# Moving the four copies of kept scores within the even steps of a fused top-k attention and MLP kernel

## The chip, the cores and the metric

The kernel runs on one core of one Trainium2 chip (trn2). The metric is the device time of one execution in microseconds (us). The engines are called PE (TensorE, matrix products), DVE (VectorE), ACT (ScalarE), POOL (GpSimd) and SP (SyncE, which issues most DMAs here). PEld is PE's loading of weights. Each engine works through its own queue in order; semaphores hold an instruction until what it needs is there.

## The reference

Two blocks follow one another: attention in which each query keeps its 32 best keys, and a two-layer MLP.

```python
# q, k, v: (8, 8, 576, 64)
scores = scale * np.matmul(q, k.transpose(0, 1, 3, 2))
kth = np.partition(scores, -top_k, axis=-1)[..., -top_k:-top_k + 1]   # top_k = 32
scores = np.where(scores >= kth, scores, -1000000000.0)
scores = scores - np.max(scores, axis=-1, keepdims=True)
attn = np.exp(scores)
attn = attn / (np.sum(attn, axis=-1, keepdims=True) + 1e-09)
attn_out = np.matmul(attn, v)
# x: the heads side by side, (4608, 512)
h = x @ w_in                    # (512, 2048)
out = np.maximum(0.01 * h, h) @ w_out   # (2048, 512)
```

## The kernel before

**Units and steps.** A unit is 128 query rows for two heads (one pair), or 64 rows of two pairs where the 576 queries leave a rest. It has 2 x 576 scores in each of 128 partitions. There are 144 units, one to a step. The first four steps stand beside the loading of weights; from step 4 on, `even(s)` and `odd(s + 1)` alternate, and everything an engine does in them is issued in the order in which these two functions name it. Nothing is reordered by a planner; only the amount of MLP work in a slot (`mlp_steps(budget)`) is shared out by a cost count.

**The life of a unit.** In a step, `cur` is the unit of this step, `old` that of the step before, `older` the one before that.
- PE computes the scores of two units at a time at the end of an even step (`scores`, L237) into three PSUM tiles: two of name `wide` (352 keys of each unit) and one of name `narrow` (224 keys of both). ACT moves them to `s_sb` in the odd step (`keep_scores_of`, L246, four copies).
- DVE runs `top_k(cur)`: two elementwise operations (L310), then four rounds of MAX8 (L316) and MATCH_REPLACE8 (L321). They give the 32nd largest score of a row.
- One step later come `limits` (L331 on ACT, L332 and L333 on POOL) and `mask` (L337, ACT), then `exponents` (L340, ACT), which also sum, and `sums` (L345, `ze`). DVE takes the reciprocal `rz` (`reciprocals`, L349). ACT multiplies by it (`normalize`, L352).
- In an even step the unit before last (`older`) is normalized after the masks of `old`, and `old` itself later in the same step, after the exponentials.
- POOL takes the 32-bit weights apart into 16-bit halves (`split`, L361); SP writes the halves to DRAM (L362, twice) and reads them back transposed as `wT` (`transpose`, L366, a DMA that waits for both L362 to have landed).
- PE multiplies `wT` with the values (`values`, L405) into a spare part of a `wide` tile; ACT puts the result into `x` (L428). `x` feeds the MLP, whose pieces on PE are L445, L462, L544, L558 and L636, and whose results leave PSUM by ACT's L440, L464, L532 and L566, called by `catch_up` where the MLP's work is cut.

**Kept scores.** In the odd steps 5 to 15, `score_early` lets PE compute scores of units that come much later, from keys and queries loaded into `raw` tiles (`load_early`, L271, L276). They use the same three PSUM tiles. In the following even step, four copies on ACT (L285) bring them to SBUF and four DMAs on SP (L286) to DRAM; `fetch_scores` (L301) brings them back much later. Two functions matter here:

```python
281    def store_scores(count):
282        for _ in range(min(count, len(to_store))):
283            u, k0, k1, ps = to_store.pop(0)
284            one = raws.tile([P, 2, WIDE], F32, name="top", bufs=2)[:, :, 0:k1 - k0]
285            nc.scalar.copy(one, ps)
286            nc.sync.dma_start(kept_of[u].rearrange("p (i n) -> p i n", i=2)[:, :, k0:k1], one)
...
216    def tiles_for_scores(us):
218        narrow = ps_sc.tile([P, 2, 512], F32, name="narrow")
221            wide = ps_sc.tile([P, 2, 512], F32, name="wide", bufs=2)
```

The four copies of a step are, in order, `wide`, `narrow`, `narrow`, `wide`; here they are called copies 1 to 4. `top` has two buffers, so copy 3 uses the buffer of copy 1 and copy 4 that of copy 2. `scores(new, ...)` at the end of the same even step writes the PSUM tiles that the copies read: its order is first `wide` tile, `narrow` (16 matmuls), second `wide` tile.

In `even`, before: `store_scores(2)` stands at line 801, after the masks, and again at line 816, after `sums(old)`. The units with kept scores are those of steps 6, 8, 10, 12, 14 and 16 as far as copying goes; in the other even steps both calls find nothing to store.

Of the kernel before, what the change touches and what calls it, by code (L numbers as in the profile page):

```python
# [20 lines left out]
def kernel(  # L21
# [160 lines left out]
    def load_waiting():  # L182
        if waiting_v or waiting:
            nc.sync.dma_start(*(waiting_v or waiting).pop(0))
# [31 lines left out]
    def tiles_for_scores(us):  # L216

        narrow = ps_sc.tile([P, 2, 512], F32, name="narrow")
        ps, spare = {}, []
        for k, u in enumerate(us):  # L220
            wide = ps_sc.tile([P, 2, 512], F32, name="wide", bufs=2)
            ps[u] = ((wide[:, :, 0:WIDE], 0, WIDE),
                     (narrow[:, :, k * NARROW:(k + 1) * NARROW], WIDE, S))
            spare.append(wide[:, :, WIDE:WIDE + P])
        return ps, spare
# [55 lines left out]
    def store_scores(count):  # L281
        for _ in range(min(count, len(to_store))):
            u, k0, k1, ps = to_store.pop(0)
            one = raws.tile([P, 2, WIDE], F32, name="top", bufs=2)[:, :, 0:k1 - k0]
            nc.scalar.copy(one, ps)  # L285
            nc.sync.dma_start(kept_of[u].rearrange("p (i n) -> p i n", i=2)[:, :, k0:k1], one)  # L286
# [11 lines left out]
    def fetch_scores(u):  # L298
        u.both = work.tile([P, 2, S], F32, name="s_sb", bufs=5)
        u.s = [u.both[:, i, :] for i in range(2)]  # L300
        nc.sync.dma_start(u.both.rearrange("p i n -> p (i n)"), kept_of[u])  # L301

    def top_k(u):

        u.tops = small.tile([P, 2, ROUNDS, 8], F32, name="tops")
        pairs = work.tile([P, 2, 2, HS], F32, name="pairs", bufs=1)
        for n, op in enumerate((ALU.max, ALU.min)):
            nc.vector.tensor_tensor(pairs[:, :, n, :], u.both[:, :, 0:HS], u.both[:, :, HS:S], op)  # L310
        yield
        for r in range(ROUNDS):
            rest = [pairs[:, i, 0, :] if r < ROUNDS // 2 else
                    pairs[:, i, :, :].rearrange("p n h -> p (n h)") for i in range(2)]
            for i in range(2):
                nc.vector.max(out=u.tops[:, i, r, :], in_=rest[i])  # L316
            if r == ROUNDS - 2:
                yield
            if r + 1 < ROUNDS:
                for i in range(2):  # L320
                    nc.vector.match_replace(out=rest[i], in_to_replace=u.tops[:, i, r, :],  # L321
                                            in_values=rest[i], imm_value=LOWEST)
            yield

    def limits(u):

        largest, least_kept = u.tops[:, :, 0, 0], u.tops[:, :, ROUNDS - 1, 7]
        u.nleast = small.tile([P, 2], F32, name="nleast")
        u.nbias = small.tile([P, 2], F32, name="nbias")
        u.z = small.tile([P, 2], F32, name="z")  # L330
        nc.scalar.activation(u.nleast, least_kept, AF.Copy, bias=0.0, scale=-1.0)  # L331
        nc.gpsimd.tensor_tensor(u.nbias, least_kept, largest, ALU.subtract)  # L332
        nc.gpsimd.tensor_scalar(u.nbias, u.nbias, SCALE, None, ALU.mult)  # L333

    def mask(u, i):

        nc.scalar.activation(u.s[i], u.s[i], AF.Prelu, bias=u.nleast[:, i:i + 1], scale=1.0, alpha=BELOW)  # L337

    def exponents(u, i):
        nc.scalar.activation(u.s[i], u.s[i], AF.Exp, bias=u.nbias[:, i:i + 1], scale=SCALE,  # L340
                             accum_out=u.z[:, i:i + 1])
# [5 lines left out]
    def reciprocals(u):  # L347
        u.rz = small.tile([P, 2], F32, name="rz")
        nc.vector.reciprocal(u.rz, u.ze)  # L349

    def normalize(u, i):
        nc.scalar.activation(u.s[i], u.s[i], AF.Copy, bias=0.0, scale=u.rz[:, i:i + 1])  # L352

    def split(u):


        pairs = u.both.rearrange("p i n -> p (i n)").bitcast(U16).rearrange("p (n h) -> p n h", h=2)
        u.apart = halves.tile([P, 2, 2 * S], U16, name="apart")
        for h in range(2):
            split = work.tile([P, 2 * S], U16, name="split", bufs=2)  # L360
            nc.gpsimd.tensor_copy(split, pairs[:, :, h])  # L361
            nc.sync.dma_start(u.apart[:, h, :], split)  # L362

    def transpose(u):
        u.wT = work.tile([P, 2 * NKC - 1, P], F32, name="wT", bufs=3)
        nc.sync.dma_start_transpose(out=u.wT.bitcast(U16), in_=u.apart.rearrange("p h n -> (p h) n"))  # L366

    def transpose_in_haste(u):

        both = u.both.rearrange("p i n -> p (i n)")  # L370
        u.parts_T = []
        for c0, c1 in ((0, 8), (8, 2 * NKC - 1)):
            pt = ps_sc.tile([P, 2, 512], F32, name="wide", bufs=2)
            pt = pt.rearrange("p h (c n) -> p (h c) n", n=P)
            for c in range(c0, c1):
                nc.tensor.transpose(pt[:, c - c0, :], both[:, c * P:(c + 1) * P], ident)
            u.parts_T.append((c0, c1, pt))
# [113 lines left out]
    def send_now():  # L491
        while to_send:
            nc.sync.dma_start(*to_send.pop(0))
# [18 lines left out]
    def catch_up():  # L512
        while due:
            due.pop(0)()
# [143 lines left out]
    def mlp_steps(budget):  # L658
        owed[0] += budget
        while owed[0] > 0:  # L660
            if running[0] is None:
                if not ready:
                    owed[0] = 0.0
                    return
                running[0] = mlp(ready.pop(0))
            cost = next(running[0], None)
            if cost is None:
                running[0] = None
            else:
                owed[0] -= cost  # L670
                backlog[0] -= cost
# [12 lines left out]
    def unit(n):  # L684
        return steps[n] if FIRST <= n < len(steps) else None
# [15 lines left out]
    def slot_budget(s):  # L701

        after = [at for at, _ in ready_at if at > s]
        if len(after) >= len(CHUNKS) - EARLY:
            return EARLY_SHARE * (0.6 if s - 2 in HASTY else 1.0)
        until = after[0] if after else s + 1
        group = [GROUP * (at % 2 == 0 and at < len(steps)) for at in range(s, until)]
        return max((backlog[0] + sum(group)) / len(group) - group[0], 0.0) / SLOTS
# [5 lines left out]
    with tc.manual_schedule():  # L714
# [67 lines left out]
        def even(s):  # L782
            cur, old, older = unit(s), unit(s - 1), unit(s - 2)
            in_haste = s - 2 in HASTY
            new = [u for u in steps[s + 2:s + 4] if u]
            if new and new[0] in early_units:
                new = []
            picks = top_k(cur) if cur else iter(())
            budget = slot_budget(s)
            next(picks, None)  # L790
            if older:
                reciprocals(older)
            for _ in range(4):
                next(picks, None)
            load_waiting()
            send_now()
            if old:
                limits(old)
                mask(old, 0)
                mask(old, 1)  # L800
            store_scores(2)
            catch_up()
            if older:
                normalize(older, 0)
                normalize(older, 1)
                if not in_haste:
                    split(older)
                    transpose(older)
                else:
                    transpose_in_haste(older)  # L810
            mlp_steps(budget)
            if old:
                exponents(old, 0)
                exponents(old, 1)
                sums(old)
            store_scores(2)
            if older and in_haste:
                keep_transposed(older)
            if old:
                reciprocals(old)  # L820
            for _ in picks:
                pass
            for _ in range(4):
                mlp_steps(budget)
            if old:
                normalize(old, 0)
                normalize(old, 1)
            sum_now(2)
            mlp_steps(budget)
            mlp_steps(budget)  # L830
            if unit(s + 3) in early_units:
                fetch_scores(unit(s + 3))
            ps, spare = tiles_for_scores(new) if new else (None, [])
            weighed = values(s, spare)
            if new:
                scores(new, ps)
            load_more(s)
            return new, ps, weighed
# [221 lines left out]
```

## Time and profile before

| | us |
|---|---|
| median of 3 runs | 1443.55 (1441.15 to 1444.76) |
| profiled execution | 1442.51 |
| its span | 1440.7 |
| mean granted PE clock | 0.981 |

| L285 and L286, the copies of kept scores and their DMAs | |
|---|---|
| L285 copies | 12 `wide` of 0.75, 12 `narrow` of 0.53, from 125.8 to 225.6 us |
| L286 DMAs | 24, from 126.5 to 231.3 us, 2.8 us from issue to landing in the median (2.5 to 3.7) |

How to read the profile's lines: a timeline line gives the start in us from the span's start, the duration, the engine, the line of the kernel, the operation, what is written <- what is read, and the count; in brackets the idle time of the engine just before, and what ended it. SPq is SP's queue issuing a DMA. A line of the waits names engine, tile and line that waited, what released it, the total in us, the times, and the longest. A busy share is a mean over stages with different limits; a wait's price is read in its own stage.

### The profile page before, as it was taken

To read this page: it belongs to the slowest core of one execution; us is meant where nothing else is said; L and a number is where in the kernel's file an instruction comes from. 1 tells how busy PE (TensorE), PEld (TensorE's weight loads), DVE (VectorE), ACT (ScalarE), POOL (GpSimd) and SP (SyncE) were. 2 spreads that over 40 slices of the span, in tenths; PEclk is the share of its full clock that TensorE was granted. 3 is DMA by queue.
4 is the path that set the end of the run, shared out by engine and by line. 5 is a ranking of instruction groups with operands and counts; after the bars stand their busy time and mean duration, and the time that the engine had idled before them with its cause. 6 is when DMAs were issued, how large, how long until landed. Compare 5 with 4: busy or idle time off the path is not lost.

```text
span 1440.7 us, 27849 instructions
## 1 busy us (share of the span) xinstructions
PE 1350.1 (94%) x9794; PEld 1031.2 (72%) x9794; DVE 1321.4 (92%) x3412; ACT 1025.3 (71%) x2144; POOL 714.3 (50%) x796
## 2 busy tenths in 40 slices
PE   5679799969999999999999999999999999999998
PEld 2234454438778888878788888878778888888887
DVE  7989998999999999999999999999999999999700
ACT  6877877767677777767777777767677777777621
POOL 2332335435646464655555555555655555555512
PEclk9899899989999999999999999999999999999999
DMA  7683766665767656675676567766765565555400
GB/s 301 229 269 114 221 181 191 180 182 132 190 182 170 159 141 188 184 199 128 197 196 179 142 146 182 201 178 151 201 176 165 149 159 143 167 141 139 127 12 15
DMA packets 410239, 241.64 MB, mean 168 GB/s; under 512 B 340080, under 2 KB 356977, under 8 KB 408177
## 3 DMA queue, kind: packets, MB, share of 16 engines
q1 hardware_dynamic: 408944, 238.80, 60.5%
q8 instruction: 77, 1.26, 0.4%
q10 hardware_dynamic: 1152, 1.05, 0.2%
q14 instruction: 66, 0.53, 0.1%
HBM read 55.77 MB, written 100.27 MB: 108 GB/s over the span
## 4 chain that ended last, share of the span: by engine, by line
DVE 67%; PE 19%; issue 6%; ACT 4%; DMA 2%; POOL 1%; DVEq 0%; SPq 0%; POOLq 0%
DVE tops L316 32%; DVE pairs L321 25%; DVE pairs L310 7%; PE ph L544 5%; PE pz L558 4%; PE ph L445 3%; PE wide L405 2%; PE pz L636 1%; PE wide L237 1%; DVE rz L349 1%; ACT s_sb L340 1%; ACT s_sb L352 1%; DMA apart<-split 1%; PE narrow L237 1%; DMA wT<-apart 1%
## 5 line engine op out<-in xcount | busy, mean ns | idle before, releaser
L316 DVE MAX8 tops<-pairs 128x8 f32<-128x288 f32 (+1 forms) x1152 | 636.6, 593 | 0.3 <-DVE rz L349 0.3
L544 PE MATMUL ph<-x,w_in 128*128 128x256 f32 x2048 | 458.5, 383 | 7.8 <-ACT gT L532 6.9
L321 DVE MATCH_REPLACE8 pairs<-tops,pairs 128x288 f32<-128x288 f32 (+1 forms) x864 | 460.9, 539 | 0.0
L544 PEld LDWEIGHTS ph<-x,w_in 128*128 128x128 f32 x2048 | 384.8, 190 | 86.5 <-issue 16.3
L361 POOL COPY split<-s_sb 128x1152 uint16<-128x1152 uint16 x284 | 317.5, 1147 | 206.1 <-ACT s_sb L352 206.1
L352 ACT ACTIVATE s_sb<-s_sb,rz 128x576 f32<-128x576 f32 x288 | 207.0, 767 | 140.7 <-DVE rz L349 139.9
L332 POOL TENSOR_TENSOR nbias<-tops 128x2 f32<-128x2 f32 x144 | 73.8, 513 | 385.2 <-DVE tops L316 381.6
L558 PE MATMUL pz<-w_out,gT 128*128 128x256 f32 x1024 | 226.8, 379 | 0.8 <-POOL gT L483 0.8
L310 DVE TENSOR_TENSOR pairs<-s_sb 128x576 f32<-128x576 f32 x288 | 214.4, 784 | 12.4 <-ACT s_sb L261 2.0
L340 ACT ACTIVATE s_sb<-s_sb,nbias 128x576 f32<-128x576 f32 x288 | 223.6, 784 | 0.0
L558 PEld LDWEIGHTS pz<-w_out,gT 128*128 128x128 f32 x1024 | 194.2, 190 | 28.4 <-POOL gT L483 2.0
L337 ACT ACTIVATE s_sb<-s_sb,nleast 128x576 f32<-128x576 f32 x288 | 207.6, 768 | 4.7
L405 PE MATMUL wide<-wT,vt 128*64 128x128 f32 (+1 forms) x2560 | 157.0, 284 | 24.9 <-DMA wT<-apart 22.2
L405 PEld LDWEIGHTS wide<-wT,vt 128*64 128x64 f32 (+1 forms) x2560 | 128.5, 138 | 62.9 <-issue 39.0
L558 PE MATMUL pz<-raw,top 128*128 128x256 f32 x512 | 116.6, 383 | 3.5 <-ACT o_sb L566 3.5
L558 PEld LDWEIGHTS pz<-raw,top 128*128 128x128 f32 x512 | 95.4, 190 | 24.9 <-issue 4.7
L237 PE MATMUL wide<-kt,qt 64*64 64x352 f32 x1040 | 101.6, 461 | 0.0
L246 ACT COPY s_sb<-wide 128x704 f32<-128x704 f32 x130 | 99.1, 762 | 3.2 <-PE wide L237 3.2
L532 ACT ACTIVATE gT<-ph 128x512 f32<-128x512 f32 x128 | 75.4, 589 | 32.8 <-PE ph L544 32.8
L333 POOL TENSOR_SCALAR nbias<-nbias 128x2 f32<-128x2 f32 x144 | 84.4, 586 | 12.6
L331 ACT ACTIVATE nleast<-tops 128x2 f32<-128x2 f32 x144 | 28.6, 199 | 86.8 <-DVE tops L316 85.9
L566 ACT COPY o_sb<-pz 128x256 f32<-128x256 f32 x112 | 41.9, 374 | 67.3 <-PE pz L558 67.2
(76 smaller groups left out, 1257.3 us busy)
## 6 DMA issues: line engine op xcount, KB each, us to landing
apart<-split SPq DMA_DIRECT2D x284, 288.0 KB, 2.2
raw<-in_weights_dram SPq DMA_DIRECT2D x15, 1024.0 KB, 6.2
vt<-in_vk_dram SPq DMA_DIRECT2D x32, 320.0 KB, 3.7
qt<-in_qT_dram SPq DMA_DIRECT2D x32, 288.0 KB, 3.5
kt<-in_kT_dram SPq DMA_DIRECT2D x32, 288.0 KB, 4.0
out_dram<-o_sb SPq DMA_DIRECT2D x64, 128.0 KB, 2.4
s_sb<-kept SPq DMA_DIRECT2D x12, 576.0 KB, 4.3
kept<-top SPq DMA_DIRECT2D x12, 352.0 KB, 2.9
```

Of the source, the lines that this page charges most:

```text
L237: nc.tensor.matmul(to[r0:r0 + LEFT, i, :], qt[d, q0 - left:q0 - left + LEFT], kt[d, k0:k1], start=True, stop=True)
L246: nc.scalar.copy(u.both[:, :, k0:k1], to)
L310: nc.vector.tensor_tensor(pairs[:, :, n, :], u.both[:, :, 0:HS], u.both[:, :, HS:S], op)
L316: nc.vector.max(out=u.tops[:, i, r, :], in_=rest[i])
L321: nc.vector.match_replace(out=rest[i], in_to_replace=u.tops[:, i, r, :], in_values=rest[i], imm_value=LOWEST)
L337: nc.scalar.activation(u.s[i], u.s[i], AF.Prelu, bias=u.nleast[:, i:i + 1], scale=1.0, alpha=BELOW)
L340: nc.scalar.activation(u.s[i], u.s[i], AF.Exp, bias=u.nbias[:, i:i + 1], scale=SCALE, accum_out=u.z[:, i:i + 1])
L352: nc.scalar.activation(u.s[i], u.s[i], AF.Copy, bias=0.0, scale=u.rz[:, i:i + 1])
L361: nc.gpsimd.tensor_copy(split, pairs[:, :, h])
L405: nc.tensor.matmul(po[n * D:(n + 1) * D, side, 0:P], v_of[u.pairs[0]][k, at, side, :], u.wT[k, at + side * NKC if at + 1 < NKC else at, :] ...
L544: nc.tensor.matmul(ph[:, i, 0:n], w_in[c][:, f * P:(f + 1) * P], x[:, c, 0:n], start=(c == 0), stop=(c == HP - 1),)
L558: nc.tensor.matmul(to, g[:, f, :], w(f), start=(first and f == 0), stop=(f == HALF - 1), skip_group_check=not first)
```

## The change

Two calls of `store_scores(2)` remain, in other places. The one behind the masks is taken out. The one behind `sums(old)` stays, and now carries copies 1 and 2. A new one stands at the end of the even step, after `normalize(old)`, the last MLP slots and `fetch_scores`, ahead of `tiles_for_scores(new)`, and carries copies 3 and 4. Copies, sizes, buffers and tiles are as before.

```diff
@@ -798,7 +798,6 @@
                 limits(old)
                 mask(old, 0)
                 mask(old, 1)
-            store_scores(2)
             catch_up()
             if older:
                 normalize(older, 0)
@@ -830,6 +829,7 @@
             mlp_steps(budget)
             if unit(s + 3) in early_units:
                 fetch_scores(unit(s + 3))
+            store_scores(2)
             ps, spare = tiles_for_scores(new) if new else (None, [])
             weighed = values(s, spare)
             if new:
```

In the changed program's order of instructions, PE, DVE and POOL have the same sequence as before. On ACT the L285 move as said. On SP the four L286 of a step stand together, behind the two L362 and the L366 of the even step; before, two stood ahead of these and two behind.

## Prediction

> **What bounds the kernel now.** I read the page first: engine totals, then the chain of work that ended last, then the list of who waited for whom on VectorE (DVE), then the timeline of the stretch that the change touches.
>
> ```profile
> PE 1350.1 (94%) x9794; PEld 1031.2 (72%) x9794; DVE 1321.4 (92%) x3412; ACT 1025.3 (71%) x2144; POOL 714.3 (50%) x796
> ...
> DVE 67%; PE 19%; issue 6%; ACT 4%; DMA 2%; POOL 1%; DVEq 0%; SPq 0%; POOLq 0%
> ```
>
> ```profile
> DVE rz L349 <- ACT ze L345: 21.2, 11, 8.0
> ```
>
> Two thirds of the chain is DVE's top-k. From about 300 us the chain is an unbroken run of L316/L321 pairs (one step each 8.8 us) until DVE has no more work, then TensorE (PE) drains to the end at 1440.7. In 300 to 320 us PE itself idles for the transposed weights, so PE follows DVE there: a delay of DVE ahead of 300 us moves everything behind it. What DVE waits for is almost only `rz`, the reciprocal, on ScalarE's (ACT) `ze`. The copies of kept scores (L285) run only in the even steps 6, 8, 10, 12, 14 and 16, between 125 and 232 us. Step 6, in the timeline:
>
> ```profile
> 125.75 0.75 ACT L285 COPY top<-wide 128x704 f32<-128x704 f32 x1 [2.52 <-PE wide L237]
> ...
> 128.93 2.23 POOL L361 COPY split<-s_sb 128x1152 uint16<-128x1152 uint16 x2 [6.51 <-ACT s_sb L352]
> ...
> 130.10 1.44 SPq L362 DMA_DIRECT2D apart<-split  x2
> ...
> 130.52 0.52 ACT L285 COPY top<-narrow 128x448 f32<-128x448 f32 x1
> 130.64 0.17 DVE L349 RECIPROCAL rz<-ze 128x2 f32<-128x2 f32 x1 [1.65 <-ACT ze L345]
> ...
> 133.43 2.60 SPq L366 DMA_TRANSPOSE wT<-apart  x1
> ...
> 136.12 1.20 SPq L286 DMA_DIRECT2D kept<-top  x2
> ```
>
> See two things. First, copy 1 stands ahead of the exponentials and waits 2.52 for PE; DVE then waits 1.65 for `ze`. Second, SP's queue is in order: copies 3 and 4 ended at 131.6, but their stores (L286) were issued at 136.12, when the transpose (L366) ahead of them, itself waiting for the split to land, had gone. In step 8 even the first stores stood behind a transpose:
>
> ```profile
> 143.21 2.58 SPq L366 DMA_TRANSPOSE wT<-apart  x1
> ...
> 145.84 1.24 SPq L286 DMA_DIRECT2D kept<-top  x2
> ...
> 148.85 0.53 ACT L285 COPY top<-narrow 128x448 f32<-128x448 f32 x1 [1.04 <-DMA kept<-top]
> ```
>
> Copy 3 writes the buffer of copy 1 (`top` has two), and started 3.0 us after copy 1's store was issued: ACT waited for a DMA.
>
> **What the change removes.** No instruction is added or dropped; PE, DVE and POOL keep their order, ACT and SP change theirs. Copies 1 and 2 leave the place ahead of `ze`. DVE's mid-step waits for `ze` in the six steps are 1.65, 0, 0, 0.30, 1.35 and 3.15: 6.45 us at most to be won. In step 6: the matmuls for L440 end at 124.93, so L440 and the two L352 (0.49 + 1.44) end at 126.9 instead of 128.9, `ze` at 128.6, and DVE, free at 128.99, waits for nothing. What is late next is below.
>
> **What it moves onto the path.** On SP the order becomes L362 x2, L366, then all four L286. So every first store now stands behind a transpose, as in step 8. Call N the end of the older unit's two normalizations (L352) in an even step. From N to the L286 behind that transpose the six steps of before took 7.25, 7.45, 7.18, 6.97, 7.17 and 7.12 us: 7.2. The landing of such a store is 2.5 to 3.7, and 3.0 and 2.8 where a first store stood behind a transpose: 2.9, and 0.1 for the start. Copy 3 thus starts at N + 10.2, though ACT is there at about N + 5 (exponentials and `ze` 1.75, copies 1.3, L352 1.45). Copies 3 and 4 take 0.53 + 0.75: over at N + 11.5.
>
> Queued behind copy 3 on ACT: the odd step's `nleast` and masks (1.65 by 133.38 to 134.98), L428 and the four L246, the exponentials, `ze`. On PE: scores(new) needs the `narrow` bank (copy 3) and the second `wide` bank (copy 4); PE came to it at 132.94 in step 6 and now waits until about 137.6. Its 16 + 8 matmuls end by N + 12.5, before ACT reads them, so PE is not the longer arm. DVE waits for that `ze` at the next even step's `rz`. From the first of L428/L246 to the end of `ze` the odd steps took 4.48, 4.27, 4.42, 4.78, 4.28, 4.77; in the fourth and sixth an L440 of 0.5 stands ahead. So `rz` follows at N + 17.5 to 18.5. Then ACT needs `nleast`, masks and L352 (3.1) to the next N; two L440 add 1.1 from step 10 to 12, the sends at L628 and an L440 add 2.05 from 14 to 16. From N to N: 20.7, 20.5, 21.8, 21.5, 22.6, against 17.65 that DVE's two steps take. ACT and SP now set the pace, and DVE idles 3 to 5 us in each double step.
>
> **The sum.** N in step 6 is 126.9; adding up, step 16 has 234.0, and `rz` at the start of step 18 comes at 234.0 + 18.5 = 252.5. Before:
>
> ```profile
> 240.08 0.17 DVE L349 RECIPROCAL rz<-ze 128x2 f32<-128x2 f32 x1 [0.59 <-ACT ze L345]
> ```
>
> That is +12.4 us; the waits of before in this stretch are replaced by the longer loop, so the gain is already in it. From step 18 there are no copies, and PE, ACT and DVE are late by 12.0 to 12.6 alike, so later waits stay. Profiled execution: 1442.5 + 12.4 = 1454.9 (span 1440.7 and 1.8 around it). It lies 1.0 under the median of the runs, 1443.55, which gives 1455.9. I say **1455.5**.
>
> **Unknown sizes.** How copy 3 waits is not in this order in the trace. If no wait came, all six waits would be won: -6.45. With the fastest rows (6.97 and 2.5) a step is 0.6 shorter: +8.8; with the slowest (7.45 and 3.7) 1.05 longer: +18.7. I take the middle because the 7.2 repeats within 0.3. Later, DVE's waits of 1.85 and 0.50 at 287 and 299 us could be won if PE comes there relatively earlier: -2.4. The DVE adds at 248 us, stretched to 4.77 for two beside a POOL addition (1.43 elsewhere), could meet POOL otherwise: 3.3 either way. The other reordered pieces (gT copies, L440, loads at the end of the step) cost nothing: ACT idles 5 us ahead of copy 3, and loads are due steps later; without that cover each costs its 0.5.
>
> **Clock.** PE will idle about 4 us per even step. In this trace an idle of 3.75 us at 152 to 156 was followed by half clock:
>
> ```profile
> 148.00:150.00 2.00, 2.00 (x34) 1.00 1.02 373
> ...
> 156.00:158.00 2.00, 1.99 (x19) 0.50 1.06 399
> ...
> 164.00:166.00 2.00, 2.00 (x22) 0.50 0.65 240
> ```
>
> (Columns: window, busy PE, granted clock, DMA share, GB/s.) The 38 matmuls of L405 took 4.31 instead of 2.34. Scores at half speed end 1.5 us later, still hidden: ACT reads `narrow` at N + 13.9. From scores(new) of step 10 to those of step 12 PE has 19.7 us of work in 21.8, so there a slow clock shows: 0 to 4 us in all. I keep 0 for the forecast and 4 for the range. The Trainium skill, "TensorE: Matmul & The Clock Gate", Part 1, says that the clock halves after an idle window of about 3.4 us whose grid runs freely, so that a gap of 4 us may or may not meet one; as an estimate by that page, one window per gap would be 1.7 us of PE time each, 10 in all, mostly inside PE's slack. The trace's 156 us case agrees with a halving; no row shows how often it will happen.
>
> A rule speaks for the change: the skill's "Trainium Kernel Development and Optimization", Best Practices, wants double buffering to overlap DMA with compute, and `top` is double-buffered. By that rule alone the stores would be hidden and the sum would be -6.45; the 1.04 at 148.85 shows two buffers not to be enough when the store's issue is held up.
>
> **Rivals.** (1) *Faster*: copy 3 does not wait. The mechanism is the earlier `ze`: DVE wins 1.65, 0.30, 1.35 and 3.15, and the end comes at 1436 to 1437. It decides if the first stores land before N + 5; for it speaks that in steps 12 to 16 of before no store was behind a transpose, against it the order of SP's queue in the changed program. Chance 0.06. (2) *Absorbed*: the wait exists but ACT's idle time, 29% of the span, swallows most. For 0 to +6 copy 3 would have to start 1.1 to 2.1 us earlier than N + 10.2 (12.4 over six steps is 2.1 each), or part is won back at 248 to 300 us: 1443 to 1449. Chance 0.12, of which 0.05 within 0.3%. (3) *Worse*: PE at half clock reaches scores(new) after ACT. If each stall brings three slow windows, as at 156 to 171 (10.2 us slow, 5.1 lost), it passes PE's slack by 5 at step 12 and 1 or so elsewhere: +8 on top, 1463 to 1466. Chance 0.12. (4) Forecast, +6 to +20: 0.70.
>
> **How the numbers follow.** The range 1448.5 to 1463 is the forecast with the bounds (+8.8 - 2.4, and +18.7, and 1.0 between profile and median), and leaves out about 0.2. Some 0.3% (4.3 us) is what a measurement here can tell from no change: faster 0.06, same 0.05, slower 0.89.
>
> **What would show it.** ACT's L285 waiting for "DMA kept<-top" six times, about 5 us each, where before has one of 1.04. PE waiting for L285 at `narrow` L237, about 4 us, six times. DVE's wait for `ze` gone in mid-step and 3 to 5 us at each even step's first `rz`, the total at 30 to 36 instead of 21.2; step 18's `rz` near 252.5. After 300 us, the same pattern shifted. I am wrong if L285 shows no DMA wait, if L286 is issued ahead of L366, or if the shift at 300 us is not that at the end.

## The result, and the profile after

The changed kernel takes 1458.71 us in the median of 5 runs (1457.56 to 1460.76), before 1443.55 (1441.15 to 1444.76): ratio 1.0109, 95% interval 1.0094 to 1.0124. The profiled execution took 1458.71 with a span of 1456.9, so 16.2 more than the 1440.7 of before. The forecast was 1455.5, range 1448.5 to 1463.

The page of the changed kernel, engine totals and chain by engine:

```profile
PE 1354.6 (93%) x9794; PEld 1032.2 (71%) x9794; DVE 1320.1 (91%) x3412; ACT 1025.2 (70%) x2144; POOL 711.0 (49%) x796
...
DVE 65%; PE 16%; issue 6%; ACT 6%; DMA 4%; POOL 2%; SPq 1%; ACTq 0%; DVEq 0%; POOLq 0%
```

DVE and ACT do no more work than before (1321.4 and 1025.3 there). PE's 4.5 us more for the same 9794 matmuls are slower matmuls: the mean granted clock of this execution is 0.978 instead of 0.981. What is new is in the chain: ACT 6% instead of 4, DMA 4% instead of 2, and SP's queue with 1%. Who waited for whom (total, times, longest):

```profile
DVE rz L349 <- ACT ze L345: 29.4, 14, 8.0
...
ACT top L285 <- DMA kept<-top: 28.7, 8, 5.5
...
PE narrow L237 <- ACT top L285: 12.6, 4, 4.4
PE wide L405 <- ACT top L285: 5.3, 1, 5.3
...
DVE pairs L310 <- ACT s_sb L246: 12.0, 7, 2.9
```

The copies wait 28.7 us for DMAs, where before has 1.0 in all. DVE's waits for ACT (L349 and L310 together) are 41.4 instead of 22.4. Step 6 in the timeline of the changed kernel:

```profile
125.38 1.43 ACT L352 ACTIVATE s_sb<-s_sb,rz 128x576 f32<-128x576 f32 x2
...
128.60 0.17 DVE L349 RECIPROCAL rz<-ze 128x2 f32<-128x2 f32 x1 [0.32 <-ACT ze L345]
...
129.10 0.54 ACT L285 COPY top<-narrow 128x448 f32<-128x448 f32 x1
...
131.40 2.51 SPq L366 DMA_TRANSPOSE wT<-apart  x1
...
134.00 1.26 SPq L286 DMA_DIRECT2D kept<-top  x2
...
136.97 0.53 ACT L285 COPY top<-narrow 128x448 f32<-128x448 f32 x1 [5.51 <-DMA kept<-top]
137.56 1.56 PE L237 MATMUL narrow<-kt,qt 64*64 64x224 f32 x16 [4.12 <-ACT top L285]
...
140.99 1.43 DVE L310 TENSOR_TENSOR pairs<-s_sb 128x576 f32<-128x576 f32 x2 [2.19 <-ACT s_sb L246]
...
144.79 0.17 DVE L349 RECIPROCAL rz<-ze 128x2 f32<-128x2 f32 x1 [2.38 <-ACT ze L345]
```

Read it downwards. The first line ends at N, 126.81 here. The wait of 1.65 in mid-step shrank to 0.32: that is the gain. Then the two stores leave SP at 134.00, right behind the transpose, though their copies had ended at 129.6; copy 3 starts when the first has landed, 5.5 us after ACT was ready; PE and DVE wait in turn. The end of the same story, the first `rz` of step 18:

```profile
255.01 0.17 DVE L349 RECIPROCAL rz<-ze 128x2 f32<-128x2 f32 x1 [1.89 <-ACT ze L345]
```

The stretch can be measured by itself: from the first `rz` of step 6 (122.93 before, 122.21 after) to that of step 18 it takes 117.15 us before and 132.80 after, +15.65. That leaves 0.6, as a balance, for the whole rest of the span. Since this start scatters from 121.8 to 125.3 in the profiles, with the loading of weights ahead of it, the stretch is what the runs below are compared by, called S. S is read in one execution of each kernel, and PE's clock enters it too, as is seen at e10.

### The profile page after: what moved, and what is told of

It reads as the page before. It is cut to its first block, busy times and chain, and to the rows that moved or that the text cites. A ratio compares the mean times of both kernels' runs of the same rounds, so it can differ in the third digit from the quotient of the medians.

```text
span 1456.9 us, 27857 instructions
## 1 busy us (share of the span) xinstructions
PE 1354.6 (93%) x9794; PEld 1032.2 (71%) x9794; DVE 1320.1 (91%) x3412; ACT 1025.2 (70%) x2144; POOL 711.0 (49%) x796
## 4 chain that ended last, share of the span: by engine, by line
DVE 65%; PE 16%; issue 6%; ACT 6%; DMA 4%; POOL 2%; SPq 1%; ACTq 0%; DVEq 0%; POOLq 0%
DVE tops L316 31%; DVE pairs L321 24%; DVE pairs L310 7%; PE ph L544 4%; PE pz L558 4%; PE ph L445 2%; PE wide L405 2%; PE pz L636 1%; DMA apart<-split 1%; DMA raw<-in_weights_dram 1%; DMA kept<-top 1%; ACT s_sb L340 1%; PE wide L237 1%; POOL split L361 1%; ACT s_sb L246 1%
## 5 line engine op out<-in xcount | busy, mean ns | idle before, releaser
L310 DVE TENSOR_TENSOR pairs<-s_sb 128x576 f32<-128x576 f32 x288 | 212.9, 779 | 23.2 <-ACT s_sb L246 12.0
L405 PE MATMUL wide<-wT,vt 128*64 128x128 f32 (+1 forms) x2560 | 156.8, 284 | 27.1 <-DMA wT<-apart 20.7
L405 PEld LDWEIGHTS wide<-wT,vt 128*64 128x64 f32 (+1 forms) x2560 | 128.6, 138 | 64.6 <-issue 39.7
L246 ACT COPY s_sb<-wide 128x704 f32<-128x704 f32 x130 | 99.2, 763 | 1.8 <-PE wide L237 1.8
L331 ACT ACTIVATE nleast<-tops 128x2 f32<-128x2 f32 x144 | 28.7, 199 | 81.9 <-DVE tops L316 80.9
```

Source lines behind the costliest of these rows:

```text
L246: nc.scalar.copy(u.both[:, :, k0:k1], to)
L405: nc.tensor.matmul(po[n * D:(n + 1) * D, side, 0:P], v_of[u.pairs[0]][k, at, side, :], u.wT[k, at + side * NKC if at + 1 < NKC else at, :] ...
```

## The experiments

The theory: copy 3 waits for its buffer, that is for the store of copy 1, and this store stands on SP's in-order queue behind the transpose. Rival 1: the late place of copies 3 and 4 hurts by itself (PSUM is free later, the odd step starts later on ACT). Rival 2: copies 1 and 2 behind `ze` hold the `wide` bank, and so the weighted values and PE's clock. Each ratio is to runs of the kernel before on the same chip.

**Four places instead of two, no order changed (e1_own_buffers).** Copies 2 and 3 share one buffer, copy 4 goes to columns of `gT` that are idle until 358 us.

```diff
-            one = raws.tile([P, 2, WIDE], F32, name="top", bufs=2)[:, :, 0:k1 - k0]
+            n = stored[0] % 4
+            stored[0] += 1
+            keep = kept_of[u].rearrange("p (i n) -> p i n", i=2)[:, :, k0:k1]
+            if n == 3:
+                one = gT[:, 0:8, P:P + WIDE // 4].rearrange("p (i a) n -> p i a n", i=2)
+                ps = ps.rearrange("p i (a n) -> p i a n", a=4)
+                keep = keep.rearrange("p i (a n) -> p i a n", a=4)
+            elif n == 0:
+                one = raws.tile([P, 2, WIDE], F32, name="top", bufs=2)
+            else:
+                if n == 1:
+                    two[0] = raws.tile([P, 2, 2, NARROW], F32, name="top", bufs=2)
+                one = two[0][:, n - 1]
             nc.scalar.copy(one, ps)
-            nc.sync.dma_start(kept_of[u].rearrange("p (i n) -> p i n", i=2)[:, :, k0:k1], one)
+            nc.sync.dma_start(keep, one)
```

> The changed kernel, with four places for the four copies of an even step: copy 1 in one top buffer, copies 2 and 3 in the two halves of the other, copy 4 in columns of gT that nothing uses before 358 us. Orders on all queues stay those of the changed kernel. Theory (copy 3 waits for the store of copy 1, which stands on SP behind the transpose): the 28.7 us that ACT waits at the copies for DMA go to about 0, copy 3 starts at N + 5 instead of N + 10.2 (N: end of the older unit's normalization), the first rz of step 18 comes 12 to 16 us earlier than 255.0, and the time is 1437 to 1444. Rival 1 (the place at the end of the even step is what hurts: PSUM is free later and the odd step's ACT work starts later, whatever the DMA does): 1450 to 1459. Rival 2 (copies 1 and 2 behind ze hold the wide bank, and with it the weighted values and TensorE's clock): still above 1452.

Measured: 1441.70, ratio 0.9976 (0.9964 to 0.9988); S 117.41. Copy 3 in step 6, with N at 128.74 (`kernel.py` is 13 lines longer here, so L285 is L298):

```profile
133.27 0.54 ACT L298 COPY top<-narrow 128x448 f32<-128x448 f32 x1
```

It starts at N + 4.5, with no idle time ahead of it. No copy waits for a DMA any more, and that alone takes the whole loss away, with every queue in the order of the changed kernel. Rival 1 falls: copies 3 and 4 stand as late as before the edit. Rival 2 has something left, one wait of 6.5 us of PE for copy 1 at L405, but it does not make the kernel slower than before.

**The transpose behind the first stores (e8_transpose_behind).** SP's queue alone changes.

```diff
                     split(older)
-                    transpose(older)
...
             store_scores(2)
+            if older and not in_haste:
+                transpose(older)
             if older and in_haste:
```

> The changed kernel with one thing moved on SP's queue alone: the even step's transpose is issued behind the stores of copies 1 and 2 instead of ahead of them. ACT, PE, DVE and POOL keep the changed kernel's order. Theory: the first store is issued at about N + 3 and lands by N + 6, so copy 3 waits about 1 us instead of 5; the transpose itself, which waits for the split to land at N + 4.5, is not late; the time is 1438 to 1446. Rival 1 and rival 2: no instruction of ACT has moved, so 1452 to 1459.

Measured: 1438.73, ratio 0.9964 (0.9952 to 0.9976); S 114.22. Its timeline in step 6, and its waits:

```profile
134.06 1.27 SPq L286 DMA_DIRECT2D kept<-top  x2
...
135.92 2.67 SPq L366 DMA_TRANSPOSE wT<-apart  x1
...
136.90 0.53 ACT L285 COPY top<-narrow 128x448 f32<-128x448 f32 x1 [0.94 <-DMA kept<-top]
```

```profile
ACT top L285 <- DMA kept<-top: 4.5, 6, 1.2
```

The stores now leave ahead of the transpose. N is 131.3 here, so the transpose starts at N + 4.6, as early as in before, and copy 3 starts at N + 5.6 instead of N + 10.2. The wait of 28.7 has become 4.5. Buffers, copies and ACT's order are those of the changed kernel: SP's order is the cause. And this version is faster than the kernel before.

**One half of the change alone (e2_second_move): copies 1 and 2 behind the masks, 3 and 4 at the end of the step.**

```diff
                 mask(old, 1)
+            store_scores(2)
             catch_up()
...
                 sums(old)
-            store_scores(2)
```

(against the changed kernel)

> One half of the change alone: copies 1 and 2 stay behind the masks, copies 3 and 4 go to the end of the even step. The first stores then stand on SP ahead of the split and the transpose of the older unit. Theory: copy 3 finds its buffer free but for step 8, where an earlier transpose stands ahead; VectorE's mid-step waits of before (1.65, 0.30, 1.35, 3.15) stay; 1441 to 1447. Rival 1 (the late place hurts by itself): 1450 or more. Rival 2 (the first pair's move hurts): as before, 1443 plus or minus 2, so it is not told from the theory here.

Measured: 1442.58, ratio 0.9995 (0.9985 to 1.0004); S 118.91. No copy waits for a DMA, since the first stores now stand ahead of the split. DVE's mid-step waits stay, 3.40, 0, 0, 2.18, 1.34 and 3.14; the first is 1.8 longer than in before, behind half clock (0.50 from 106 to 108 us) that before did not have there; the fourth is 1.9 longer, and why was not looked for. The second move alone neither wins nor loses.

**The other half alone (e3_first_move): all four copies behind `ze`.**

```diff
                 sums(old)
-            store_scores(2)
+            store_scores(4)
...
-            store_scores(2)
             ps, spare = tiles_for_scores(new) if new else (None, [])
```

(against the changed kernel)

> The other half alone: copies 1 and 2 go behind ze as in the changed kernel, and copies 3 and 4 stay where they were before, right behind ze. Theory: copy 3 again waits for a store that stands behind the transpose, until N + 10.2, and now the normalization of the old unit (1.45) stands behind it on ACT as well, so the loop gets some 1.5 us longer in each of six steps: 1462 to 1470. Rival 1 (the end of the step is what hurts): not slower than before by more than 2, 1440 to 1446. Rival 2: 1452 to 1459, as the changed kernel.

Measured: 1484.03, ratio 1.0278 (1.0262 to 1.0294); S 157.72. Much slower, and 14 to 22 more than the theory had said. The timeline in step 12 tells why:

```profile
207.86 0.53 ACT L285 COPY top<-narrow 128x448 f32<-128x448 f32 x1 [6.56 <-DMA kept<-top]
...
209.13 0.60 ACT L440 ACTIVATE scale<-ph 128x512 f32<-128x512 f32 x1
...
209.79 4.64 PE L445 MATMUL ph<-w_in,x 128*128 128x512 f32 x5 [8.06 <-ACT scale L440]
...
220.88 1.43 DVE L310 TENSOR_TENSOR pairs<-s_sb 128x576 f32<-128x576 f32 x2 [10.42 <-ACT s_sb L246]
```

I had counted only the normalization behind copy 3. L440 stands behind it too, and PE's next MLP block waits for the PSUM that L440 empties: 8.06 us. PE's other work, down to the scores of the next units, comes later by that, and DVE waits 10.42 for them. The two arms add up instead of lying side by side.

**The same with four places (e6_first_move_own).** The edits of e3 and e1 together.

> The first move alone (all four copies behind ze), with four places for the four copies, so that no copy waits for a store. Theory (in the first move alone the wait for the store is also what costs, and L440 and L464 behind copy 3 pass it on to TensorE): the 42.6 us at the copies go to 0, TensorE's waits of 8 to 9 us for L440 in steps 12 and 16 go, and the time falls from 1484 to 1436 to 1444. Rival (the pile of four copies ahead of the normalization of the old unit costs by itself): above 1450.

Measured: 1445.01, ratio 1.0009 (0.9996 to 1.0022); S 116.21 in a profile of 1440.99. It falls by 39 us, so the wait for the store is what costs in e3 too. The time is 1 us above what I had said: of ten runs three lie at 1441.0 to 1441.5 and seven at 1444.2 to 1447.1. What parts these groups is open; the granted clock was 0.980 to 0.984 in the three and 0.976 to 0.981 in the seven.

**The stores on ACT's queue (e4_stores_on_act).** `nc.scalar.dma_start` in place of `nc.sync.dma_start` at L286.

> The changed kernel with the stores of kept scores issued from ACT's queue instead of SP's, each right behind its copy. Theory (SP's in-order queue holds the store, not the DMA engines): the store of copy 1 is issued at about N + 3 and lands by N + 6, copy 3 waits 0 to 1.5 us; ACT pays some 0.4 to 0.8 us for each issue, 2 to 3 us in a step, most of it in its idle time: 1439 to 1449. Rival (the transpose's packets in the DMA engines delay the store's landing, whoever issues it): copy 3 still starts near N + 10, 1454 to 1462.

Measured: 1446.44, ratio 1.0022 (1.0011 to 1.0033); S 120.12. The copies wait 2.3 us for DMAs in all. So the transpose's packets are not what holds the store back, its place on SP is. ACT's price shows in its timeline, copy 1 to copy 2:

```profile
129.94 0.73 ACT L285 COPY top<-wide 128x704 f32<-128x704 f32 x1
...
130.70 0.58 ACTq L286 DMA_DIRECT2D kept<-top  x1
131.32 0.53 ACT L285 COPY top<-narrow 128x448 f32<-128x448 f32 x1 [0.66 <-ACT top L285]
```

Copy 2 starts 0.66 us after copy 1 has ended, 0.58 of it the issue: ACT does nothing else meanwhile.

**The changed kernel once more (after_again), and a filler for PE.** In the changed kernel the double step from 10 to 12 took 24.16 us from N to N where the forecast had 21.8. The timeline shows L440 waiting 1.57 and 1.27 for PE there.

> The changed kernel once more, on the chip that runs the next ones, as their measure: 1457 to 1460.

Measured: 1459.45, ratio 1.0108 (1.0089 to 1.0127); S 132.85, the double step 24.03.

The filler, e7_filler:

```diff
+            if s == 10:
+                for _ in range(10):
+                    nc.tensor.matmul(ps[new[0]][0][0][:, 0, :], w_in[0][:, 0:P], w_in[1][:, 0:WIDE],
+                                     start=True, stop=True)
             if new:
                 scores(new, ps)
```

> The changed kernel with ten added matmuls of 352 columns (3.2 us of PE) in step 10 alone, ahead of scores(new), written to a PSUM place that the scores then overwrite. They fill the 3.46 us in which PE waits for copy 3 there. Theory of the missing 2.4 us (the double step from 10 to 12 took 24.2 instead of the 21.8 forecast because PE ran at half clock after its idle times, and ACT's L440 then waited 1.57 and 1.27 for PE): the clock stays full from 179 us on, the 16 matmuls of L445 take 7.1 instead of 8.6, the double step takes 21.8 to 22.5, and the time falls by 1.5 to 2.5 against the changed kernel. Rival (PE simply has too much work there, the clock adds nothing): the added work makes it 0 to 3 slower.

Measured: 1459.72, ratio 1.0113 (1.0096 to 1.0131); S 134.22, the double step 24.01: no gain. The estimate of the filler was wrong: each matmul is two passes of 0.31, the ten took 6.18 us, and the scores came 3 us late by them. L445 did take 7.13, but the run decides nothing. So it was cut to four matmuls (e10_short_filler, `range(4)`):

> The filler of the run before, cut to four added matmuls (eight passes of 0.31, 2.5 us), so that it ends before copy 3 is over. Theory of the half clock: the scores of step 10 and the 16 matmuls of L445 run at full speed (0.94, 0.77 and 7.1 us instead of 1.77, 1.39 and 8.6), L440's waits of 1.5 and 1.3 shrink to under 0.5 together with the double step from 10 to 12 (from 24.1 to 22 us), and the time falls by 1.5 to 2.5 against the changed kernel. Rival (these 16 matmuls hold L440 even at full speed): the double step loses under 1 us and the time is the changed kernel's within 1.

Measured: 1456.13, ratio 1.0089 (1.0075 to 1.0104), 2.6 under the first and 3.3 under the second measurement of the changed kernel, a little more than said. By ratios it is 0.002 less, with intervals that overlap. The double step took 21.66, L440 waited 0.18 at most. PE's lines, first of the changed kernel, then of this one:

```profile
179.69 1.77 PE L237 MATMUL narrow<-kt,qt 64*64 64x224 f32 x16 [3.46 <-ACT top L285]
181.23 1.39 PE L237 MATMUL wide<-kt,qt 64*64 64x352 f32 x8
182.56 8.64 PE L445 MATMUL ph<-w_in,x 128*128 128x512 f32 x16
```

```profile
177.86 2.72 PE L837 MATMUL wide<-w_in,w_in 128*128 128x352 f32 x8
...
182.15 0.99 PE L237 MATMUL narrow<-kt,qt 64*64 64x224 f32 x16 [0.81 <-ACT top L285]
182.99 0.82 PE L237 MATMUL wide<-kt,qt 64*64 64x352 f32 x8
183.74 7.13 PE L445 MATMUL ph<-w_in,x 128*128 128x512 f32 x16
```

The same matmuls take 11.8 us without and 8.9 with the filler. The granted clock, in windows of 2 us, was 0.50 from 180 to 184 in the changed kernel and 1.00 in the one with the filler:

```profile
182.00:184.00 2.00, 2.00 (x10) 0.50 1.03 386
```

```profile
182.00:184.00 2.00, 1.85 (x25) 1.00 0.33 111
```

S of this execution, though, is 132.88, no shorter than the changed kernel's, and its 1458.45 us are the slowest of the six runs. Of the 2.5 us won in the double step 2.1 were lost ahead of the filler: from the first `rz` of step 6 to N it took 6.27 us instead of 4.60, from 6 to 8 21.32 instead of 20.85. The loss at step 6 is half clock too. PE ahead of step 6, first in the changed kernel, then in this one:

```profile
104.93 2.34 PE L405 MATMUL wide<-wT,vt 128*64 128x128 f32 x38 [2.73 <-DMA wT<-apart]
107.20 7.13 PE L445 MATMUL ph<-w_in,x 128*128 128x512 f32 x16
```

```profile
105.10 3.11 PE L405 MATMUL wide<-wT,vt 128*64 128x128 f32 x38 [2.82 <-DMA wT<-apart]
108.14 7.95 PE L445 MATMUL ph<-w_in,x 128*128 128x512 f32 x16
```

From 106 to 108 us the clock was 1.00 in the first and 0.60 in the second: 1.6 us lost. So what the filler does for the double step is shown; that it makes the whole kernel faster rests on the medians.

The Trainium skill, "TensorE: Matmul & The Clock Gate", Part 1, has the clock fall after an idle window of about 3.4 us. The 3.46 us idle in step 10 would agree, but the runs also show half clock after much shorter ones. PE waits for the same L440 behind step 20 in every kernel; before and the changed kernel:

```profile
269.53 1.98 PE L445 MATMUL ph<-w_in,x 128*128 128x512 f32 x4 [1.85 <-ACT scale L440]
271.45 2.55 PE L417 MATMUL wide<-wT,vt 128*64 128x64 f32 x80
```

```profile
283.79 3.02 PE L445 MATMUL ph<-w_in,x 128*128 128x512 f32 x4 [1.86 <-ACT scale L440]
286.74 3.12 PE L417 MATMUL wide<-wT,vt 128*64 128x64 f32 x80
```

The clock was 1.00 from 270 to 274 in before, and 0.65 and 0.50 from 284 to 288 in the changed kernel: 1.6 us lost after an idle of 1.86. The L445 of this place were slow in after_again, e1, e7, e8 and e10 too, and not in e2, e3, e4, e6 and e9. So an idle of 3.4 us is not needed here, and the length of one idle does not decide.

**Both remedies (e9_transpose_behind_own):** the edits of e8 and e1.

> Both remedies together: the even step's transpose behind the first stores, and four places for the four copies. The 4.5 us that ACT still waited at the copies with the first remedy alone go, but VectorE waited for none of them after the first step, so by the theory the time is that of the first remedy within 2: 1437 to 1441. If copies still set the pace somewhere, it is 2 to 4 faster than that: 1434 to 1437.

Measured: 1437.02, ratio 0.9955 (0.9939 to 0.9971); S 113.11. Within the 2 us of e8 that the theory had said. It is the fastest version tried, 6.5 us under the kernel before and 21.7 under the changed one, though e8 with its two moved lines has nearly all of it. What makes it 4.7 us faster than e1, whose copies wait for no DMA either, was not tried. In the two profiles the double step from 10 to 12 took 22.0 us in e1 and 18.1 here, and half clock lasted until 172 us in e1 and until 167 here.

## Why the prediction was right

**Bound, right.** S grew by 15.65, the span by 16.2: a delay of DVE in the stretch moves everything behind it. The shift is 15.85 us at 300 us and 16.2 at the end.

**The gain, mostly right.** The mid-step waits of 1.65, 0, 0, 0.30, 1.35 and 3.15 became 0.32, 0, 0, 3.94, 0 and 0.61. The forecast won the fourth too; there the slow clock, below, pushed N and with it `ze`: 1.17 are left in e10. The first is won only at full clock. It is 0 to 0.48 where the clock stayed at 1.00 between 104 and 112 us (the changed kernel twice, e4, e6), and 1.59 to 2.00 where it fell to 0.50 to 0.55 there (e1, e3, e7 to e10). That the gain exists, about half as large as the 6.45 of the forecast, is shown by e8 and e9: mid-step waits of 3.3 are left, and S is 2.9 and 4.0 shorter than in before. In e1, with half clock at both places, waits of 6.2 are left and S is not shorter.

**The stores behind the transpose, right.** From N to L286 the six steps took 7.19, 7.40, 7.04, 6.96, 6.86 and 7.05 us; the forecast was 7.2. Copy 3 started at N + 10.16, 11.34, 10.11, 10.65, 9.86 and 10.00; the forecast was 10.2. In step 8 the landing took 3.9 us, more than any that the forecast's rows had; why was not tried.

**The pace, right but for two terms.**

| N to N | forecast | measured |
|---|---|---|
| 6 to 8 | 20.7 | 20.85 |
| 8 to 10 | 20.5 | 21.33 |
| 10 to 12 | 21.8 | 24.16 |
| 12 to 14 | 21.5 | 21.65 |
| 14 to 16 | 22.6 | 22.02 |
| 16 to `rz` of 18 | 18.5 | 18.19 |

The sum is 128.2 instead of 125.6. Two terms are 3.2 too small, the others 0.6 too large together. One of the two is the slow landing in step 8 (0.8). The other is the clock, which the forecast had named for exactly this double step, with 0 to 4 us, and put at 0: it was 2.4, as the double step of e10 shows. N in step 6 came where the forecast had it (126.81 for 126.9), though the first `rz` of this step was 0.7 early.

There was one more idle of PE that the forecast had not seen: 5.30 for copy 1 at L405, because the weighted values lie in the `wide` tile that copy 1 now empties later. The clock fell behind it as well (0.50 from 170 to 174 us). This did not lengthen the double step: e10 has the same idle (5.04) and 0.50 from 172 to 178, and takes 21.66.

**Behind step 18, missed.** The first `rz` of step 18 was late by 14.9 instead of 12.4, and the forecast kept this lateness to the end. It fell to 14.3 at step 20 and rose to 15.85 at step 22, where `rz` waits 1.40 for `ze` and did not in before. That is the half clock behind the idle of 1.86 shown at e10; in e4, e6 and e9, which had full clock there, it does not come. Another 0.4 came at step 80, and why was not looked for. The changed kernel has this stretch in both of its profiles and the kernel before not in its one. How often it comes in each is not known from so few, so its share in the 15.2 us between the medians is open.

The range as stated, 1448.5 to 1463, is a little wider than its own terms give (1448.9 to 1462.2).

**Where the waits show, half right.** The forecast put all of DVE's wait at `rz`. In fact DVE meets L310 first, which needs the L246 behind copy 3: 12.0 us stand there, and only 29.4 instead of 30 to 36 at `rz`. PE's waits for copy 3 at `narrow` were 4.12, 4.41 and 3.46 in steps 6 to 10 and 0 to 0.64 afterwards, not 4 in all six: PE, by then late itself, came to the scores after the copies.

**Rivals.** "Faster" is what e1, e8 and e9 do: with the wait gone the end is 1437 to 1442, and its forecast was 1436 to 1437. That e9 comes so near is in part luck, since about half of the waits that it was to win are still there. "Absorbed" did not come. Of "worse", PE at half clock, one double step had 2.4 us, not the 8 that it named.

**The rule of double buffering** (the Trainium skill, "Trainium Kernel Development and Optimization", Best Practices) was no guard here. Two buffers were enough in before, where they waited 1.04 once, and not enough once the store's issue stood behind a transpose; e8 gets by with two.

## What to carry to other kernels

A buffer is not free because its DMA is short, but when its DMA has been issued and has landed: in the changed kernel the issue came 7 us behind N and the landing 3 us behind that. Before copies are moved, list what stands ahead of their stores on the issuing queue in the new order. Then list what stands behind the waiting instruction on its engine, MLP evictions included: in e3 such an unrelated eviction turned a wait of 6.6 into one of 10.4 on another engine. Here the cheaper remedy was not another buffer but the order of two DMA issues.

## What the runs showed of the hardware

- Between 120 and 260 us a transpose issue held SP's queue for 2.2 to 2.8 us, and before that SP waited for the split to land; in e4 a plain store issue on ACT's queue cost ACT about 0.6 us each.
- The stores' landing ranged from 2.4 to 4.7 us in the changed kernel (median 2.8), so a forecast from the median misses single steps by up to 1 us in the case seen (step 8).
- A filler of 2.7 us of matmuls without a use saved PE 2.9 us of half clock and its double step 2.4 to 2.5; the median is about 3 us lower. One of 6.2 us saved nothing.
- Half clock came after an idle of PE of 1.85 or 1.86 us in six profiles, and not after 1.84 to 2.01 us at the same place of the program in the six others. It cost 1.6 to 1.7 us each time. In the nine runs of e8 the time goes roughly with the mean granted clock, from 1436.33 us at 0.984 to 1442.69 at 0.978.
